# The first phase of an FFT-filter and bilinear kernel put into one list of single steps

## The chip, the cores and the metric

The kernel runs on one core of a Trainium2 chip. The metric is the time of one execution on the device, in microseconds. PE is TensorE, DVE is VectorE, ACT is ScalarE, POOL is GpSimd and SP is SyncE, which here only issues transfers.

## The reference

```python
X = np.fft.rfft(x, axis=1)                 # x: (8, 3072, 256) float32
F = (filt_r + 1j * filt_i)[None, :, :]
y = np.fft.irfft(X * F, n=3072, axis=1).astype(np.float32)
h = y.reshape(8 * 3072, 256)
out = ((h @ w_a) * (h @ w_b) @ w_out).astype(np.float32)   # d_ff = 1536
```

The three weights arrive as float64, 8 bytes per element.

## The kernel before

**The main loop.** A batch (3072 rows) is worked on as 6 chunks (c) of 4 x 128 rows, and each chunk against 6 pairs of column blocks (p). `pair` does one of these 288 units. It makes seven products per weight (`term`, L577, three matmuls each, a high and a low part of every operand), adds them on VectorE (`add`, L627), multiplies the two sides (`g`, L649, L652, L661), splits `g` into a high part on ScalarE and a low part on GpSimd (`parts`, L586), and multiplies it by `w_out` in the next unit (`project`, L594). While a batch is in this loop, the FFT of the next one is put between the units by `plan` and `early`, two tables of slots; a unit has two slots.

**The first phase** is what must come ahead of the first unit: the FFT, the filter and the inverse FFT of batch 0, and as many weights as are needed at once. It is written in lines 684 to 723.

- Stage one has 12 steps: `first_x` loads 256 KB of x, `first_s1` multiplies it by a table on TensorE, ScalarE copies the result out of PSUM (L483) into one of two buffers `z`, and ScalarE's queue stores it to DRAM (L484).
- Stage two has 16 steps, which read DRAM in another order, so every store of stage one must have landed: `first_z` loads 192 KB (L494), `first_f` a tile of the filter (L488, real rows in partitions 0 to 63, imaginary rows in 64 to 127), `first_s2` multiplies by a table (L500), then by the filter. On VectorE that is two multiplications of 64 rows by the real part (L510, L511) and one by the imaginary part (L512). The fourth goes over ScalarE (L513, a negated copy) and GpSimd (L514). `first_is1` transforms back and stores 192 KB to `td`.
- `first_tt` (L535) loads the part of `td` that the first unit needs, and `is2` (L544) makes the first chunk from it, with L548 as its first matmuls.

**The weights** come as 18 items of 512 columns, in threes: `w_a`, `w_b` and `w_out` for each p. An item is loaded as raw words (`conv_load`, 512 KB), and its float64 bits are turned into a float32 value and a remainder. `conv_expo` masks the exponent (VectorE), `conv_scale` makes a power of two from it (ScalarE, twice, in PSUM), `conv_parts` does four operations on VectorE, `conv_split` adds the low word on GpSimd, `conv_combine` makes four sums of blocks on VectorE (L304, only for `w_a` and `w_b`), copies the high part on ScalarE and subtracts it on GpSimd. `more_weights` calls all six for six successive items; one call is a tick.

```python
for stage, lag in ((conv_combine, 5), (conv_split, 4), (conv_parts, 3), (conv_scale, 2), (conv_expo, 1), (conv_load, 0)):
    if 0 <= t - lag < len(conv):
        stage(conv[t - lag])
```

Fifteen ticks stand in the first phase. The other eight stand in slots 0 to 7 of batch 0 (L740 to L742), one in each slot, that is in the first four units.

**What sets the order.** `tc.manual_schedule()` takes the instructions as they are written: each engine works through its own in that order, and waits where an operand or a buffer isn't ready. The transfers of SP go out in their written order too, and a transfer that waits for a buffer holds back those behind it.

## Time and profile before

| | us |
|---|---|
| median of 3 runs | 2661.36 (2660.98 to 2662.94) |
| the profiled execution, its own time | 2662.36 |
| its span, first to last instruction | 2660.6 |
| busy: PE, DVE, ACT, POOL | 2589.5, 1665.2, 1412.2, 1321.8 |

The page of the profile gives shares over the whole span. The change lies in the first 180 us, so the views by window, by group and by time of that stretch are the ones to read. In the timeline a line is one instruction or a run of the same, with its start, its length, and in brackets how long the engine was idle ahead of it and what ended that.

### The profile page before, as it was taken

What the parts mean: (1) busy time and instruction counts of PE and PEld (TensorE: products, weight loads), DVE (VectorE), ACT (ScalarE), POOL (GpSimd) and SP (SyncE); (2) the same over time, 40 slices, a digit from 0 to 9 for tenths busy, and PEclk for the clock granted to TensorE, in tenths of its full rate; (3) what the DMA queues carried; (4) which work ended last, traced back from release to release, by engine and by line L of the source; (5) the groups of instructions that cost most, each with busy time, mean ns of one, the idle gap of its engine ahead of it and who ended that gap; (6) DMA issues with size and microseconds to landing.
All of it is one profiled execution on the core that took longest, in us unless ns stands there. A gap on an engine that the chain in (4) does not pass through costs nothing.

```text
span 2660.6 us, 54030 instructions
## 1 busy us (share of the span) xinstructions
PE 2589.5 (97%) x20920; PEld 2518.2 (95%) x20920; DVE 1665.2 (63%) x2648; ACT 1412.2 (53%) x2630; POOL 1321.8 (50%) x1044
## 2 busy tenths in 40 slices
PE   5789999999999999999999999999999999999999
PEld 2389999999999999999999999999999999999998
DVE  5775785558845687456865478545884468744443
ACT  3456555555555555555555555555555555545444
POOL 3575454545545555454545545454454545434333
PEclk6899999999999999999999999999999999999999
DMA  7626441344324443244423454234432444311000
GB/s 248 181 98 223 141 135 62 127 150 137 113 74 136 158 137 97 78 163 136 145 66 112 139 154 139 66 119 156 132 120 66 144 152 141 94 33 33 29 21 17
DMA packets 213634, 310.88 MB, mean 117 GB/s; under 512 B 21393, under 2 KB 121298, under 8 KB 213330
## 3 DMA queue, kind: packets, MB, share of 16 engines
q1 hardware_dynamic: 184882, 278.85, 32.7%
q10 hardware_dynamic: 28496, 28.58, 3.5%
q8 instruction: 164, 2.69, 0.4%
q14 instruction: 92, 0.75, 0.1%
HBM read 202.49 MB, written 108.00 MB: 117 GB/s over the span
## 4 chain that ended last, share of the span: by engine, by line
PE 88%; POOL 4%; DVE 3%; issue 2%; DMA 2%; ACT 1%; SPq 0%; ACTq 0%; POOLq 0%; DVEq 0%
PE po L603 10%; PE ps_p L582 10%; PE ps_p L583 9%; PE ps_p L584 9%; PE po L601 9%; PE po L602 9%; PE ps_r L584 5%; PE ps_r L582 5%; PE ps_r L583 5%; PE ps L548 3%; PE ps_q L582 2%; PE ps_q L584 2%; PE ps_q L583 2%; PE ps L361 2%; POOL xol L567 2%
## 5 line engine op out<-in xcount | busy, mean ns | idle before, releaser
L591 POOL TENSOR_TENSOR gl<-g,gh 128x512 fp32r<-128x512 f32 x576 | 747.1, 1297 | 959.2 <-ACT gh L590 894.7
L601 PE MATMUL po<-woh,gh 128*128 128x256 f32 x2304 | 656.1, 285 | 0.0
L603 PE MATMUL po<-woh,gl 128*128 128x256 f32 x2304 | 649.7, 282 | 3.1 <-POOL gl L591 1.1
L590 ACT CAST gh<-g 128x512 fp32r<-128x512 f32 x576 | 358.9, 623 | 550.6 <-DVE g L649 532.0
L602 PE MATMUL po<-wol,gh 128*128 128x256 f32 x2304 | 645.9, 280 | 0.0
L627 DVE TENSOR_TENSOR cs<-ps_r,s 128x512 f32<-128x512 f32 x288 | 199.1, 691 | 450.6 <-PE ps_r L584 397.0
L623 ACT COPY s<-ps_p 128x512 f32<-128x512 f32 x576 | 338.0, 587 | 242.5 <-PE ps_p L584 205.9
L603 PEld LDWEIGHTS po<-woh,gl 128*128 128x128 f32 x2304 | 433.8, 188 | 7.8 <-POOL gl L591 7.8
L601 PEld LDWEIGHTS po<-woh,gh 128*128 128x128 f32 x2304 | 434.9, 189 | 3.1
L602 PEld LDWEIGHTS po<-wol,gh 128*128 128x128 f32 x2304 | 434.7, 189 | 2.9
L582 PE MATMUL ps_p<-xoh,wah 128*128 128x256 f32 x1152 | 326.0, 283 | 12.0 <-DVE cs L627 7.6
L584 PE MATMUL ps_p<-xol,wbh 128*128 128x256 f32 x1152 | 323.9, 281 | 0.0
L583 PE MATMUL ps_p<-xoh,wal 128*128 128x256 f32 x1152 | 323.6, 281 | 0.0
L584 PE MATMUL ps_p<-xol,wah 128*128 128x256 f32 x1152 | 323.1, 280 | 0.0
L582 PE MATMUL ps_p<-xoh,wbh 128*128 128x256 f32 x1152 | 322.7, 280 | 0.0
L583 PE MATMUL ps_p<-xoh,wbl 128*128 128x256 f32 x1152 | 322.6, 280 | 0.0
L627 DVE TENSOR_TENSOR cs<-ps_q,s 128x512 f32<-128x512 f32 x288 | 199.1, 691 | 187.0 <-PE ps_q L584 161.4
L649 DVE TENSOR_TENSOR g<-cs 128x512 f32<-128x512 f32 x288 | 300.9, 1045 | 6.1 <-POOL gl L591 6.1
L567 POOL TENSOR_TENSOR xol<-xf,xoh 128x256 fp32r<-128x256 f32 x192 | 246.9, 1307 | 20.9 <-ACT xoh L566 20.9
L661 DVE TENSOR_TENSOR g<-ps_p,cs 128x256 f32<-128x256 f32 x288 | 122.1, 424 | 213.2 <-ACT cs L660 210.2
L442 POOL TENSOR_TENSOR yl<-y,yh 128x512 fp32r<-128x512 f32 x112 | 144.3, 1289 | 223.7 <-ACT yh L441 223.7
L582 PEld LDWEIGHTS ps_p<-xoh,wah 128*128 128x128 f32 x1152 | 217.5, 189 | 13.8 <-DVE cs L627 8.5
(125 smaller groups left out, 6239.1 us busy)
## 6 DMA issues: line engine op xcount, KB each, us to landing
filt<-in_filt SPq DMA_DIRECT2D x336, 128.0 KB, 2.8
z<-zh SPq DMA_DIRECT2D x112, 256.0 KB, 3.0
zt<-z SPq DMA_DIRECT2D x112, 256.0 KB, 3.0
td<-t ACTq DMA_DIRECT2D x128, 192.0 KB, 2.2
out<-ot SPq DMA_DIRECT2D x95, 256.0 KB, 2.1
tt<-td SPq DMA_DIRECT2D x47, 512.0 KB, 4.2
xt<-in_x SPq DMA_DIRECT2D x84, 256.0 KB, 2.9
st<-s1d SPq DMA_DIRECT2D x84, 256.0 KB, 3.4
```

What stands on the lines that cost most here:

```text
L567: nc.gpsimd.tensor_tensor(out=xl[:, o], in0=xf[:, i], in1=f32(xh[:, o]), op=ALU.subtract)
L582: nc.tensor.matmul(o, wh[:, p, w], xh[:, i], start=first and h == 0, stop=False, skip_group_check=True)
L583: nc.tensor.matmul(o, wl[:, p, w], xh[:, i], start=False, stop=False, skip_group_check=True)
L584: nc.tensor.matmul(o, wh[:, p, w], xl[:, i], start=False, stop=True, skip_group_check=True)
L590: nc.scalar.copy(out=gh, in_=g[:, f])
L591: nc.gpsimd.tensor_tensor(out=gl, in0=g[:, f], in1=f32(gh), op=ALU.subtract)
L601: nc.tensor.matmul(o, gh[:, ts], woh[:, n], start=n == 0 and j % 2 == 0, stop=False, skip_group_check=True)
L602: nc.tensor.matmul(o, gh[:, ts], wol[:, n], start=False, stop=False, skip_group_check=True)
L603: nc.tensor.matmul(o, gl[:, ts], woh[:, n], start=False, stop=n == NF - 1, skip_group_check=True)
L623: nc.scalar.copy(out=s, in_=bank)
L627: nc.vector.tensor_tensor(out=cs[:, :, n], in0=bank, in1=s, op=ALU.add)
L649: nc.vector.tensor_tensor(out=g[:, 0].rearrange("p (t n) -> p t n", t=2), in0=cs[:, 0, 0:2], in1=cs[:, 1, 0:2], op=ALU.mult)
```

## The change

- **One list.** The first phase is no longer written as loops with ticks between, but as `FIRST`, a list of 289 single steps in one order. A letter is a function, the number its item or step: `g x k s z w` are stage one (`z` the copy out of PSUM, `w` the store, now issued by SP), `Z f S y n v I t T` stage two, `r o a c h l j q` the eight steps of one weight item. Items 0 to 11 are done in it, and items 12 to 15 are loaded.
- **Conversion.** `conv_open` masks the exponent and, in a second operation with two scalars, takes the mantissa and sets its leading bit, then adds the low word times 2^-32 (L275). `conv_close` puts the sign into the scale and multiplies (two operations). The addition on GpSimd and two operations on VectorE go; the four block sums move from VectorE to GpSimd (L326).
- **Filter.** The real filter is loaded into both halves of the rows (`filt_r`, 256 KB), the imaginary part into rows 64 to 127 (`filt_i`, 128 KB). VectorE does one multiplication of 128 rows (L555) and one of 64 (L556). The later batches load the filter in this layout too, with two transfers where there were three.
- **Buffers.** The result of stage one has one place in SBUF for all 12 steps, in memory that weights use later; 13 input tiles instead of 8; five sets of filter tiles for steps 0 to 9, two for the rest.
- **Main loop.** Items 12 to 17 are opened in slots 0, 1, 3, 4, 6 and 7 and done by slot 9, over five units.

```diff
+FIRST = """
+g0 x0 x1 x2 r0 g1 x3 x4 x5 r1 s0 g2 x6 x7 s1 z0 x8 r2 s2 z1 w0 g3 o0 z2 w1 x9 w2 x10 s3 x11 a0 k s4 r3 s5 z3
...
+w10 o3 w11 l2 j1 q1 a3 c3 h3 Z0 l3 f0 Z1 f1 Z2 S0 f2 j3 Z3 n0 Z4 q3 y0 Z5 S1 Z6 Z7 v0 n1 Z8 y1 Z9 S2 Z10 v1
+Z11 I0 n2 y2 Z12 r4 v2 f3 I1 t0 f4 T0 r5 f5 I2 t1 f6 T1 r6 S3 f7 S4 r7 n3 Z13 o4 S5 Z14 n4 Z15 S6 v3 y3 v4 a4
...
+c10 r13 h9 t15 l9 o11 r14 h10 T15 a11 j9 c11 q9 r15 h11 l10 l11 j10 q10
+"""
...
+    def conv_open(w):
...
+        v.tensor_scalar(out=e, in0=hw, scalar1=0x7FF00000, scalar2=None, op0=ALU.bitwise_and)
+        v.tensor_scalar(
+            out=m, in0=hw, scalar1=0xFFFFF, scalar2=0x100000, op0=ALU.bitwise_and, op1=ALU.bitwise_or
+        )
+        v.scalar_tensor_tensor(
+            out=f32(m), in0=lw.bitcast(U32), scalar=2.0 ** -32, in1=m, op0=ALU.mult, op1=ALU.add
+        )
...
+    def conv_close(w):
+        raw, _, m, sc = w[3:]
+        nc.vector.scalar_tensor_tensor(
+            out=sc, in0=raw[:, :, 1], scalar=-(1 << 31), in1=sc, op0=ALU.bitwise_and, op1=ALU.bitwise_or
         )
...
+        nc.vector.scalar_tensor_tensor(
+            out=f32(m), in0=f32(m), scalar=2.0 ** -20, in1=f32(sc), op0=ALU.mult, op1=ALU.mult
         )
...
-    def conv_split(w):
...
-        nc.gpsimd.tensor_tensor(out=m, in0=m, in1=f32(dst_h), op=ALU.subtract)
-        nc.gpsimd.tensor_tensor(out=dst_l, in0=m, in1=f32(lo), op=ALU.add)
...
-            nc.vector.tensor_tensor(out=s[:, o], in0=a, in1=b, op=op)
...
+            nc.gpsimd.tensor_tensor(out=s[:, o], in0=a, in1=b, op=op)
...
+        nc.sync.dma_start(out=z0[:, 2 * i:2 * i + 2], in_=firsts["z"][:, 2 * i:2 * i + 2])
...
+        n = i % 5 if i < 10 else i % 2
...
+        nc.sync.dma_start(out=fr_, in_=filt_r[:, 2 * i:2 * i + 2])
+        nc.sync.dma_start(out=fm[64:128], in_=filt_i[:, 2 * i:2 * i + 2])
...
-        nc.vector.tensor_tensor(out=y[0:64], in0=ps[0:64], in1=ft[0:64], op=ALU.mult)
-        nc.vector.tensor_tensor(out=y[64:128], in0=ps[64:128], in1=ft[0:64], op=ALU.mult)
-        nc.vector.tensor_tensor(out=v[64:128], in0=ps[0:64], in1=ft[64:128], op=ALU.mult)
...
+        nc.vector.tensor_tensor(out=y, in0=ps, in1=fr_, op=ALU.mult)
+        nc.vector.tensor_tensor(out=v[64:128], in0=ps[0:64], in1=fm[64:128], op=ALU.mult)
...
-                left = len(conv) + 5 - tick[0]
-                for i in range(left):
-                    at(i, more_weights)
...
+                for i, t in enumerate((0, 1, 3, 4, 6, 7), len(conv) - 6):
+                    for fn, lag in zip(CONV[1:], (0, 0, 1, 1, 2, 2, 2)):
+                        at(t + lag, fn, conv[i])
+                    if i + 4 < len(conv):
+                        at(t + 2, conv_load, conv[i + 4])
```

**SP, where stage two begins.** `z_98` and `z_94` are the DRAM tensor between the stages, `raw` the words of a weight item, `filt`, `f` the filter. Before:

```order
L245 DMA raw<-in_wb 128x2x512
L494 DMA zf<-z_98 96x2x256
L488 DMA filt_95<-in_filt 128x512
L494 DMA spare<-z_98 96x2x256
L488 DMA filt_96<-in_filt 128x512
L494 DMA spare<-z_98 96x2x256 x2
L245 DMA raw<-in_wo 128x2x512
```

In the changed kernel:

```order
L529 DMA zf<-z_94 96x2x256
L537 DMA f_289<-in_fr 128x512
L538 DMA f_289<-in_fm 64x512
L529 DMA zf<-z_94 96x2x256 x5
L529 DMA spare<-z_94 96x2x256 x5
L261 DMA raw<-in_wb 128x2x512
L537 DMA f_289<-in_fr 128x512
L538 DMA f_289<-in_fm 64x512
```

After the filter tile of step 2, ten loads of `z` and a weight item now stand ahead of the filter tile of step 3; before, loads of `z` and of the filter alternated.

**VectorE, in the middle of stage two.** `y`, `v` are the products with the filter, `e`, `m`, `sc` belong to a weight item. Before:

```order
L512 TENSOR_TENSOR v_387<-ps,filt_94 64x512
L270 SCALAR_TENSOR_TENSOR sc<-raw,sc 128x512
L273 TENSOR_SCALAR m<-raw 128x512
L274 SCALAR_TENSOR_TENSOR m<-m,sc 128x512
L277 SCALAR_TENSOR_TENSOR e<-raw,sc 128x512
L250 TENSOR_SCALAR e<-raw 128x512
L510 TENSOR_TENSOR y_412<-ps,filt_95 64x512
L511 TENSOR_TENSOR y_412<-ps,filt_95 64x512
L512 TENSOR_TENSOR v_413<-ps,filt_95 64x512
```

In the changed kernel:

```order
L556 TENSOR_TENSOR v_335<-ps,f_289 64x512
L271 TENSOR_SCALAR e<-raw 128x512
L272 TENSOR_SCALAR m<-raw 128x512
L275 SCALAR_TENSOR_TENSOR m<-raw,m 128x512
L555 TENSOR_TENSOR y_395<-ps,f_289 128x512
L556 TENSOR_TENSOR v_396<-ps,f_289 64x512
L555 TENSOR_TENSOR y_400<-ps,f_289 128x512
L556 TENSOR_TENSOR v_401<-ps,f_289 64x512
L293 SCALAR_TENSOR_TENSOR sc<-raw,sc 128x512
L296 SCALAR_TENSOR_TENSOR m<-m,sc 128x512
```

A filter step takes two instructions instead of three, and an item comes in two halves with filter steps between them.

**VectorE, from one unit of the main loop to the next.** `cs` and `g` belong to the unit. Before, from the second unit to the third:

```order
L661 TENSOR_TENSOR g<-ps_p,cs 128x256
L304 TENSOR_TENSOR s<-m 128x128
L304 TENSOR_TENSOR s<-s,m 128x128
L304 TENSOR_TENSOR s<-m 128x128
L304 TENSOR_TENSOR s<-m,s 128x128
L270 SCALAR_TENSOR_TENSOR sc<-raw,sc 128x512
L273 TENSOR_SCALAR m<-raw 128x512
L274 SCALAR_TENSOR_TENSOR m<-m,sc 128x512
L277 SCALAR_TENSOR_TENSOR e<-raw,sc 128x512
L250 TENSOR_SCALAR e<-raw 128x512
L627 TENSOR_TENSOR cs<-ps_q,s 128x2x256
```

In the changed kernel, from the first unit to the second:

```order
L722 TENSOR_TENSOR g<-ps_p,cs 128x256
L293 SCALAR_TENSOR_TENSOR sc<-raw,sc 128x512
L296 SCALAR_TENSOR_TENSOR m<-m,sc 128x512
L271 TENSOR_SCALAR e<-raw 128x512
L272 TENSOR_SCALAR m<-raw 128x512
L275 SCALAR_TENSOR_TENSOR m<-raw,m 128x512
L688 TENSOR_TENSOR cs<-ps_q,s 128x2x256
L293 SCALAR_TENSOR_TENSOR sc<-raw,sc 128x512
L296 SCALAR_TENSOR_TENSOR m<-m,sc 128x512
L688 TENSOR_TENSOR cs<-ps_r,s 128x2x256
```

Between the last `g` of a unit and the first addition of the next stand five instructions instead of nine; one more item is closed ahead of the second addition.

## Rows read from the trace of the kernel before

**Rows 1.** page, section 1: busy us, share of the span, instructions of each engine

```profile
PE 2589.5 (97%) x20920; PEld 2518.2 (95%) x20920; DVE 1665.2 (63%) x2648; ACT 1412.2 (53%) x2630; POOL 1321.8 (50%) x1044
```

**Rows 2.** busy us of each engine in stretches of 20 us

```profile
core 0: us, PE busy (x) PEld busy (x) DVE busy (x) ACT busy (x) POOL busy (x), PEclk, DMA share, GB/s
60.00:80.00 20.00, 15.64 (x33) 6.48 (x32) 19.45 (x31) 8.90 (x16) 11.76 (x10) 0.84 0.66 197
80.00:100.00 20.00, 18.11 (x36) 6.51 (x34) 19.45 (x31) 10.52 (x19) 13.17 (x12) 0.87 0.81 237
...
160.00:180.00 20.00, 18.12 (x139) 17.66 (x138) 18.20 (x32) 10.11 (x22) 15.48 (x14) 0.91 0.05 11
180.00:200.00 20.00, 20.00 (x172) 20.00 (x171) 9.15 (x17) 11.28 (x23) 12.20 (x11) 1.00 0.32 106
```

**Rows 3.** timeline: start us, us, engine, line, operation; the first stage and its end

```profile
9.81 0.43 DVE L250 TENSOR_SCALAR e<-raw 128x512 int32<-128x512 int32 x1 [8.91 <-DMA raw<-in_wa]
...
34.17 0.58 ACT L483 COPY z<-ps 128x512 f32<-128x512 f32 x1 [4.89 <-DMA z<-z]
...
45.69 0.35 SPq L494 DMA_DIRECT2D zf<-z  x1
...
112.21 0.68 DVE L512 TENSOR_TENSOR v<-ps,filt 64x512 f32<-64x512 f32 x1
...
120.37 0.46 SPq L535 DMA_DIRECT2D tt<-td  x1
...
124.19 3.75 PE L548 MATMUL ps<-gt,tt 128*128 128x128 f32 x16 [6.70 <-issue]
```

**Rows 4.** waits from 0 to 130 us: us in total, times, longest

```profile
ACT z L483 <- DMA z<-z: 10.8, 5, 4.9
```

**Rows 5.** DMA from 3 to 26 us, all queues

```profile
DMA packets 4461, 8.41 MB, mean 366 GB/s; under 512 B 553, under 2 KB 778, under 8 KB 4461
```

**Rows 6.** groups by form, 0 to 125 us: busy us, mean ns, idle before

```profile
L250 DVE TENSOR_SCALAR e<-raw 128x512 int32<-128x512 int32 x14 | 11.7, 834 | 16.1 <-DMA raw<-in_wa 10.0 <-DMA raw<-in_wo 5.2 <-DMA raw<-in_wb 0.9
L510 DVE TENSOR_TENSOR y<-ps,filt 64x512 f32<-64x512 f32 x16 | 10.9, 680 | 0.3
L274 DVE SCALAR_TENSOR_TENSOR m<-m,sc 128x512 int32<-128x512 int32 x12 | 8.3, 688 | 0.4
L273 DVE TENSOR_SCALAR m<-raw 128x512 int32<-128x512 int32 x12 | 6.8, 562 | 0.1
L304 DVE TENSOR_TENSOR s<-m 128x128 f32<-128x128 f32 x14 | 4.3, 306 | 7.6 <-ACT z L483 5.1 <-POOL m L285 2.4
L307 POOL TENSOR_TENSOR wal<-m,wah 128x128 fp32r<-128x128 f32 x4 | 2.0, 491 | 13.1 <-ACT wah L305 12.9
L310 POOL TENSOR_TENSOR wal<-s,wah 128x512 fp32r<-128x512 f32 x4 | 5.3, 1313 | 0.0
```

**Rows 7.** page, section 5: VectorE on a PSUM tile of 128 rows

```profile
L627 DVE TENSOR_TENSOR cs<-ps_r,s 128x512 f32<-128x512 f32 x288 | 199.1, 691 | 450.6 <-PE ps_r L584 397.0
```

**Rows 8.** DMA issues from 0 to 130 us: KB each, median us to landing

```profile
filt<-in_filt SPq DMA_DIRECT2D x16, 256.0 KB, 3.9
```

**Rows 9.** timeline: VectorE's product g, once in each pair of column blocks

```profile
138.85 0.68 DVE L649 TENSOR_TENSOR g<-cs 128x512 f32<-128x512 f32 x1
...
176.03 1.44 DVE L649 TENSOR_TENSOR g<-cs 128x512 f32<-128x512 f32 x1
...
199.87 0.68 DVE L649 TENSOR_TENSOR g<-cs 128x512 f32<-128x512 f32 x1
```

**Rows 10.** groups by form on VectorE, 124 to 180 us

```profile
L250 DVE TENSOR_SCALAR e<-raw 128x512 int32<-128x512 int32 x4 | 5.5, 1388 | 0.0
```

**Rows 11.** timeline: two records of the second stage's matmuls

```profile
101.98 1.91 PE L500 MATMUL ps<-v,icf 128*96 128x512 f32 x2
...
103.69 1.91 PE L500 MATMUL ps<-zf,fcf 96*128 96x512 f32 x2
```

**Rows 12.** the same stretch: busy us by engine as in Rows 2, granted clock

```profile
102.00:104.00 2.00, 2.00 (x3) 0.91 (x4) 1.92 (x4) 1.21 (x3) 1.26 (x1) 0.53 0.68 198
```

More of the change, by code (lines that the diff above doesn't have):

```diff
@@ L296, in conv_combine, with conv_low @@
             return
         m = m.rearrange("p (k f c) -> p k f c", k=2, f=2)
+        wh = wt[p][:, 2 * h]
+        nc.scalar.copy(out=wh[:, 0], in_=m[:, 0, 0])
+        nc.scalar.copy(out=wh[:, 1:3], in_=m[:, 1])
+    def conv_low(w):
+        p, h, m = w[1], w[2], w[-1]
+        sub = lambda out, a, b: nc.gpsimd.tensor_tensor(out=out, in0=a, in1=f32(b), op=ALU.subtract)
+        if h is None:
+            wh, wl = (t[:, 2 * p:2 * p + 2].rearrange("p f d -> p (f d)") for t in (woh, wol))
+            sub(wl, m, wh)
+            return
+        m = m.rearrange("p (k f c) -> p k f c", k=2, f=2)
+        wh, wl = wt[p][:, 2 * h], wt[p][:, 2 * h + 1]
@@ L389, in load_f @@
         fr, fm = filts[2 * (i % 2)], filts[2 * (i % 2) + 1]
-        for h in range(2):
-            nc.sync.dma_start(out=fr[half[h]], in_=filt[half[0], 2 * i:2 * i + 2])
-        nc.sync.dma_start(out=fm[half[1]], in_=filt[half[1], 2 * i:2 * i + 2])
+        nc.sync.dma_start(out=fr, in_=filt_r[:, 2 * i:2 * i + 2])
+        nc.sync.dma_start(out=fm[half[1]], in_=filt_i[:, 2 * i:2 * i + 2])
     def load_z(b, i):
@@ L463, in first_in @@
         if not spare:
[L464 to L465 removed]
+            spare.extend(p2.tile([128, 3, 2, D], F32, name="spare", tag="xol") for _ in range(2))
+        n = taken[0] % 13
         taken[0] += 1
[L467 removed]
+        return fr.tile([128, 2, D], F32, name=name, tag="in", bufs=7) if n < 7 else spare[(n - 7) // 3][:, (n - 7) % 3]
     def first_x(i):
@@ L480, in first_s1, with first_out_z, first_turned @@
         for n in range(2):
-            nc.tensor.matmul(ps[:, n], sf[:, 2 * (i % 4) + n], xt[:, n], start=True, stop=True)
-        z = fr.tile([128, 2, D], F32, name="z0", tag="z0", bufs=2)
-        nc.scalar.copy(out=z, in_=ps)
-        nc.scalar.dma_start(out=z0[:, 2 * i:2 * i + 2], in_=z)
-    def first_f(i):
-        ft = filts[i % NFT]
-        nc.sync.dma_start(out=ft, in_=filt[:, 2 * i:2 * i + 2])
-        held["f0", i] = ft
-    def first_z(i):
+            nc.tensor.matmul(ps[:, n], sf[:, 2 * (i % 6) + n], xt[:, n], start=True, stop=True)
+        held["s0", i] = ps
+    def first_z(i):
+        if i == 0:
+            firsts["z"] = const.tile([128, 7168], F32, name="z0", tag="w45")[:, :N2 * D].rearrange("p (n d) -> p n d", n=N2)
+        nc.scalar.copy(out=firsts["z"][:, 2 * i:2 * i + 2], in_=held.pop(("s0", i)))
+    def first_out_z(i):
+        nc.sync.dma_start(out=z0[:, 2 * i:2 * i + 2], in_=firsts["z"][:, 2 * i:2 * i + 2])
+    def first_turned(i):
         zt = first_in("zf")
@@ L579, in term @@
         xh, xl = held["xo", b, c]
-        for h, (wh, wl) in enumerate(((wah, wal), (wbh, wbl))):
-            o = bank[:, h]
-            nc.tensor.matmul(o, wh[:, p, w], xh[:, i], start=first and h == 0, stop=False, skip_group_check=True)
-            nc.tensor.matmul(o, wl[:, p, w], xh[:, i], start=False, stop=False, skip_group_check=True)
-            nc.tensor.matmul(o, wh[:, p, w], xl[:, i], start=False, stop=True, skip_group_check=True)
+        for h in range(2):
+            o, wh, wl = bank[:, h], wt[p][:, 2 * h, w], wt[p][:, 2 * h + 1, w]
+            nc.tensor.matmul(o, wh, xh[:, i], start=first and h == 0, stop=False, skip_group_check=True)
+            nc.tensor.matmul(o, wl, xh[:, i], start=False, stop=False, skip_group_check=True)
+            nc.tensor.matmul(o, wh, xl[:, i], start=False, stop=True, skip_group_check=True)
     def parts(u, f):
```

213 lines of the change are left out of this document (101 added, 112 removed).

## Prediction

> **What bounds the kernel now.** I began with the shares of the whole span: TensorE is busy 97% of it [rows 1], so time can come back only where it isn't. The table of 20 us stretches says where that is [rows 2]. From 180 us on TensorE is busy 20.00 of 20 us, and only fewer matmuls could shorten that; the change leaves them alone. Ahead of it two parts are slow. From 60 to 100 us VectorE is busy 19.45 of every 20 us, and in 160 to 180 it is at 18.20, while TensorE idles there. So all that the change can win or lose lies in the first 180 us, and a microsecond by which the saturated loop starts earlier is a microsecond of the total.
>
> The timeline gives the marks [rows 3]. Stage one ends where the first load of z is issued, at 45.69; the last product with the filter ends at 112.89 (112.21 + 0.68); the first matmul of the first chunk starts at 124.19. The tail between these last two is 11.3 us. The main loop then needs until about 180 to run at its own pace.
>
> One measurement of this kernel can tell a change from none at about 0.2%, that is 5.3 us; the chances at the end use that bound.
>
> **Stage one: 45.7 to about 31 us.** What held it was the two buffers for z: ScalarE waited 10.8 us, in five waits, for a store to finish before it could copy out the next result [rows 4], one of them 4.89 us [rows 3]. All twelve results now have a place, so these waits go. What is late next is the transfers. Up to the first load of z the list moves 4 tables of 384 KB, 12 tiles of x of 256 KB, 4 weight items of 512 KB, 192 KB of small tables and 12 stores of 256 KB: 9920 KB, or 10.2 MB. From 3 to 26 us the queues moved 366 GB/s on average [rows 5], and at that rate 10.2 MB take 27.8 us. From the 3 us of the first stretch that is 31 us. The conversion of items 0 to 3 fits beside it: 4 items at the 3.5 us worked out below are 14 us of VectorE. Gain of this part: 14.7 us. The bounds: 28 us if the transfers lose nothing at the start, 36 us if the stores wait on SP behind loads as they did on ScalarE's queue half of the time.
>
> **Stage two: 67.2 us (45.7 to 112.9) to about 66.** Three resources come close together here, and I priced each.
>
> *VectorE.* A weight item took 0.83 + 3 x 0.69 + 0.56 = 3.46 us, and the sums 4 x 0.31 = 1.2 us more for two items in three [rows 6]. Now it is two masks and three operations of 0.69 us. The second mask has two scalars, which no row shows; its bounds are the 0.56 us of L273, which it replaces, and the 0.69 us of an operation with two tensors [rows 6]. I take 0.7 for each mask, so 3.5 us: the item itself isn't cheaper, only its sums leave. The filter took three operations of 0.68 us per step [rows 6]. The 128-row product is new; that 64 rows cost 0.68 and 128 rows from PSUM cost 0.69 [rows 7] says that rows are free, so a step now takes 1.38 us instead of 2.05. Eight items are left for stage two: 8 x 3.5 + 16 x 1.38 = 50 us. To that I add 8 us of idleness: ten loads of z and one item stand ahead of the filter tile of step 3, 2.5 MB, which is 8 us at the 295 GB/s below, and the three steps before it can't fill it. That gives 58 us.
>
> *Transfers.* From the first load of z to the last filter tile: 16 loads of 197 KB, 16 filter steps of 393 KB (262 before), 10 items of 524 KB, 14 stores of 197 KB and 0.65 MB for the first chunk: 18.1 MB. In stage two the queues moved 197 GB/s at a share of 0.66 and 237 at 0.81 [rows 2], so 295 GB/s at a full share; that is 61 us, and 65 us at a share of 0.95. The wider filter itself costs 2.1 MB of this, 7 us.
>
> *TensorE.* Three matmuls of 512 columns per step. At the lower of its two clock levels one took 1.71 us, the distance of two records [rows 11], where the granted clock was 0.53 [rows 12]; at the full one it takes half, 0.86. So 48 of them need 41 to 82 us, and at the 0.85 that was granted between 60 and 100 us [rows 2] about 48.
>
> The largest counts, the transfers: 65 us and one last product. Stage two alone wins a microsecond, because what VectorE gives back is asked for by the larger loads. The last product ends at 31 + 66 = 97 us, and with the old tail of 11.3 us the first chunk starts at about 108, 16 us earlier than now. The four sums that go to GpSimd cost there 4 x 0.49 us per item [rows 6], against 1.3 us for the addition that leaves it, so 0.7 us more for two items in three, and 1.3 us less for the third, where one of two subtractions goes: in total nothing. What hides it is that GpSimd was busy 13.2 of 20 us at most in this stage [rows 2]. If that cover were gone, 0.7 us would be paid for each of eight items, 5 us.
>
> **The first units of the loop.** The product g comes once in a unit. The first three intervals took 37.2 us (138.85 to 176.03), the next three 23.8 (176.03 to 199.87) [rows 9]; with the tick of some 4 us ahead of the first g about 17 us go here. VectorE takes them. In 180 to 200 us it was busy 9.15 us [rows 2] for 20/7.9 = 2.5 units, 3.6 us a unit; two ticks of 4.3 us (an item and its share of the sums) make that 12.2, and an interval was 12.4. A tick now doesn't come in every slot. Per interval the new table gives one opening and two closings, two and one, one and one, one and two, a closing being 1.4 us and an opening 0.69 us and two masks. A mask took 1.39 us here [rows 10]; for the pair I take 1.9, the second at the 0.56 of its forerunner [rows 6]. With the unit's 3.6 us that is 9.0, 10.2, 7.6 and 9.0 us. VectorE got no further than 18.20 us of work in 20 here [rows 2], a share of 0.91, so 9.9, 11.2, 8.4 and 9.9 against 7.9: 8 us lost, about 10 with the first unit. Gain: 7 us, between 2 (both masks at 1.39) and 12 (both at the 0.43 of the first one of all [rows 3]).
>
> **A rule that speaks against this.** The trace shows masks of 0.83 us on average in the first phase and of 1.39 us in the loop [rows 6, 10], so something besides their own length delays them. The Trainium skill, "SBUF — State Buffer", in the section "SBUF: two separate sides", says that VectorE, in a two-port mode or with two inputs in SBUF, and GpSimd share a pair of ports which one of them holds for a whole instruction while the other is fully blocked. By that rule two masks an item and four more operations on GpSimd are the wrong trade; the trace agrees as far as a mask's 0.43, 0.83 and 1.39 us go, and the second rival below is what it would cost if each mask met one.
>
> **The sum.** The profiled execution took 2662.4 us, 1.0 over the median of the runs and 1.8 over its span. 16 + 7 = 23 us less is 2639; against the median 2638.
>
> **Rivals.**
>
> - *The transfers go no faster than they did.* At the best 20 us of stage two, 237 GB/s [rows 2], 18.1 MB take 76 us; the first chunk starts at 120, and 4 + 7 us are won: 2650. For it: loads wait for buffers as before. Against it: more tiles, so deeper prefetch. Chance 0.15.
> - *GpSimd blocks VectorE.* If each mask waits for one 1.31 us operation of GpSimd [rows 6] on top of the 0.43 of the first mask [rows 3], the 16 masks of stage two cost 16 x 1.04 = 17 us more, VectorE needs 75 us instead of 58, 9 more than the forecast's 66, and the loop's gain is gone: 2654. For it: the masks of the loop at 1.39. Against it: in stage two VectorE was busy 97% and GpSimd some 60% [rows 2], and the mean was still 0.83. Chance 0.06.
> - *TensorE's clock stays low.* If shorter bursts keep it at the lower level, 48 x 1.71 = 82 us [rows 11] from the first z at 34 us, then a store of 3.9 us [rows 8] and the 3.8 us from the last load to the first chunk [rows 3]: the first chunk at 124, nothing won ahead of the loop and 7 us in it, 2654. Chance 0.06.
> - *VectorE paces all of it, with no idleness.* Stage two is 50 us plus 3 for the first load, the transfers keep 340 GB/s, the tail stays; the first chunk starts near 96, and with 10 us in the loop 38 us are won: 2623. Chance 0.12.
> - *One queue in single file: slower.* SP takes its list in order, and a load that waits for a buffer (only two filter sets after step 9, four item buffers) stops all behind it. A filter load lands 3.9 us after its issue [rows 8]. Each that goes out only when its user is already waiting adds that to the path. The 23 us are gone after six, and if all 16 filter loads and 10 items do it, 26 x 3.9 = 101 us stand in place of 65: 13 us slower than now, 2674. For it: the tile of step 12 needs the products of step 10 done. Against it: ten steps have five sets. Chance 0.07.
>
> **The numbers.** Forecast 2638, chance 0.54 with its bounds: stage one 5 us late and the loop's low end give 2648, stage one at 28 us and its high end 2630. The range reaches from the VectorE rival to the low clock, 2621 to 2654, and leaves out the slower rival and the far ends, about 0.15. Faster by over 0.2% is everything below 2656: the forecast, the first and fourth rival, and most of the second and third, 0.89. Within 0.2%: the rest of these two and the single file half way, 0.06. Slower: 0.05.
>
> **What would show it.** The first load of z near 31 us, the first chunk near 108, TensorE full from about 156; no wait of ScalarE for stores of z; a 128-row filter product at 0.69 us; a DMA share above 0.9 between 35 and 90 us. It is wrong if stage two gets shorter by more than 5 us (then the transfers weren't the bound), if the first load of z comes after 36, or if units still take over 12 us.

## The result, and the profile after

The changed kernel took 2677.25 us (median of 4 runs, 2674.43 to 2678.83), the kernel before 2662.15 beside it: a ratio of 1.0055, with a 95% interval of 1.0038 to 1.0073. It is 15 us slower, more than the 0.2% that a measurement can tell; 2638 was forecast. The profiled execution took 2675.81 us, its span is 2674.0.

The first phase did what was forecast of it, nearly. The timeline of the changed kernel, with the marks of [rows 3] and three of the products g of [rows 9]:

```profile
30.77 0.34 SPq L529 DMA_DIRECT2D spare<-z  x1
...
100.20 0.68 DVE L556 TENSOR_TENSOR v<-ps,filt 64x512 f32<-64x512 f32 x1
...
111.06 2.26 PE L609 MATMUL ps<-gt,tt 128*128 128x128 f32 x9 [7.29 <-DMA tt<-td]
...
123.61 0.68 DVE L710 TENSOR_TENSOR g<-cs 128x512 f32<-128x512 f32 x1
...
183.38 0.69 DVE L710 TENSOR_TENSOR g<-cs 128x512 f32<-128x512 f32 x1 [1.87 <-POOL gl L652]
...
384.64 1.52 DVE L710 TENSOR_TENSOR g<-cs 128x512 f32<-128x512 f32 x1
```

The first g comes 15.2 us earlier than before (138.85), the sixth 8.7 us earlier (183.38 against 192.10), the 29th 6.9 us earlier. That one stands in the timeline of the kernel before at

```profile
391.55 1.53 DVE L649 TENSOR_TENSOR g<-cs 128x512 f32<-128x512 f32 x1
```

At the end the lead of 6.9 us has become a lag of 13.4 (spans 2674.0 and 2660.6). So 6.5 us went in the five units from the first g to the sixth, 1.8 from there to the 29th, and 20.3 between 390 us and the end, where nothing was thought to change. The windows show that second loss. The columns are those of [rows 2]; the number in the first pair of brackets counts TensorE's products. The kernel before, 1000 to 2000 us:

```profile
1000.00:2000.00 1000.00, 997.96 (x8251) 985.28 (x8250) 653.00 (x1011) 544.47 (x1014) 507.10 (x393) 1.00 0.38 121
```

The changed kernel, with the stretches of [rows 2] ahead of it:

```profile
60.00:80.00 20.00, 13.52 (x24) 4.41 (x24) 16.92 (x23) 9.57 (x18) 13.07 (x15) 0.83 0.86 261
80.00:100.00 20.00, 14.16 (x33) 5.14 (x31) 17.19 (x22) 13.51 (x24) 15.61 (x19) 1.00 0.81 250
160.00:180.00 20.00, 16.78 (x117) 16.59 (x118) 12.61 (x20) 11.91 (x24) 13.48 (x15) 0.83 0.13 40
180.00:200.00 20.00, 18.34 (x153) 18.13 (x152) 8.46 (x15) 10.03 (x20) 10.74 (x9) 1.00 0.40 127
1000.00:2000.00 1000.00, 999.10 (x8182) 986.49 (x8181) 646.18 (x1002) 540.41 (x1004) 502.72 (x390) 1.00 0.39 121
```

TensorE is busy 99.9% of the last stretch, at the full granted clock, and completes 8182 products where it completed 8251: 0.84% fewer. Over the 2280 us after the 29th g that is 19 us, nearly all of the 20.3. Same products, same clock, no idle time, and still slower: the busy share can't show such a loss, the count in a stretch does.

Beside the filter steps of the later batches, what differs in the loop is where the operands lie. Of a product's two operands one is loaded first and held (a weight of 128x128, or a block of g), the other is streamed past it (a part of x, or of the output weights, 128x256). The compiled programs give the addresses; *modulo 512* is what is left of an address when multiples of 512 bytes are taken off. In both kernels the streamed parts of x start at byte 288 modulo 512 of their partition (124704), and g's parts at 480. The weights started at 128 (1152 and multiples of 512 from there); the new tiles are allocated as they are needed, behind the small tables, and start at 288 (38688). The output weights start at 128 in both. The runs on the rate of the loop and on the other operands move some of these.

The waits from 112 to 195 us (us in total, times, longest) tell of the first loss:

```profile
ACT w L333 <- POOL s L326: 10.6, 4, 4.7
...
PE ps_p L643 <- ACT s L684: 7.3, 2, 4.7
...
PE ps L609 <- DVE m L296: 3.3, 1, 3.3
```

Two records of the timeline belong together, ScalarE's rounding of the sums and, three instructions behind it, the copy that TensorE waits for:

```profile
139.89 0.62 ACT L333 CAST w<-s 128x512 fp32r<-128x512 f32 x1 [4.71 <-POOL s L326]
```

```profile
142.36 0.58 PE L643 MATMUL ps_p<-xoh,w 128*128 128x256 f32 x1 [4.72 <-ACT s L684]
```

### The profile page after: what moved, and what is told of

The parts are those of the page before. It is cut to its first block, busy times and chain, and to the rows that moved or that the text cites. A ratio compares the mean times of both kernels' runs of the same rounds, so it can differ in the third digit from the quotient of the medians.

```text
span 2674.0 us, 53770 instructions
## 1 busy us (share of the span) xinstructions
PE 2607.9 (98%) x20920; PEld 2539.5 (95%) x20920; DVE 1643.5 (61%) x2584; ACT 1412.7 (53%) x2630; POOL 1322.7 (49%) x1074
## 4 chain that ended last, share of the span: by engine, by line
PE 93%; DMA 3%; POOL 2%; DVE 1%; issue 1%; ACT 1%; SPq 0%; POOLq 0%; DVEq 0%; ACTq 0%
PE po L664 10%; PE ps_p L645 10%; PE po L662 10%; PE ps_p L643 10%; PE ps_p L644 10%; PE po L663 10%; PE ps_r L645 5%; PE ps_r L643 5%; PE ps_r L644 5%; PE ps L609 3%; PE ps_q L645 2%; PE ps_q L643 2%; PE ps_q L644 2%; PE ps L386 2%; PE ps L432 2%; PE ps L431 2%
## 5 line engine op out<-in xcount | busy, mean ns | idle before, releaser
L643 PE MATMUL ps_p<-xoh,w 128*128 128x256 f32 x2304 | 651.1, 283 | 10.0 <-ACT s L684 7.3
L645 PE MATMUL ps_p<-xol,w 128*128 128x256 f32 x2304 | 652.2, 283 | 0.3 <-POOL xol L628 0.3
L644 PE MATMUL ps_p<-xoh,w 128*128 128x256 f32 x2304 | 651.8, 283 | 0.0
L643 PEld LDWEIGHTS ps_p<-xoh,w 128*128 128x128 f32 x2304 | 439.8, 191 | 11.8 <-ACT s L684 8.4
L662 PEld LDWEIGHTS po<-woh,gh 128*128 128x128 f32 x2304 | 440.7, 191 | 3.0
L645 PEld LDWEIGHTS ps_p<-xol,w 128*128 128x128 f32 x2304 | 440.0, 191 | 0.5 <-POOL xol L628 0.5
L644 PEld LDWEIGHTS ps_p<-xoh,w 128*128 128x128 f32 x2304 | 440.1, 191 | 0.0
L645 PE MATMUL ps_r<-xol,w 128*128 128x256 f32 x1152 | 326.6, 284 | 1.8 <-POOL xol L628 1.8
L643 PE MATMUL ps_r<-xoh,w 128*128 128x256 f32 x1152 | 325.4, 282 | 0.0
L644 PE MATMUL ps_r<-xoh,w 128*128 128x256 f32 x1152 | 325.1, 282 | 0.0
```

Of the source, the lines that this page charges most:

```text
L643: nc.tensor.matmul(o, wh, xh[:, i], start=first and h == 0, stop=False, skip_group_check=True)
L644: nc.tensor.matmul(o, wl, xh[:, i], start=False, stop=False, skip_group_check=True)
L645: nc.tensor.matmul(o, wh, xl[:, i], start=False, stop=True, skip_group_check=True)
L662: nc.tensor.matmul(o, gh[:, ts], woh[:, n], start=n == 0 and j % 2 == 0, stop=False, skip_group_check=True)
```

## The experiments: the rate of the loop

Line numbers of a version may lie one to three above those of the changed kernel. *Distance* is the start of the streamed x less that of the held weights, modulo 512: 160 before, 0 after the change.

**Run 1, the changed kernel, weights 32 bytes further.** x comes 64 further, to 352.

```diff
-    sct = const.tile([128, 2], F32, name="sct")
+    sct = const.tile([128, 16], F32, name="sct")[:, 0:2]
             wt[p], wt[p + 1] = t[:, 0], t[:, 1]
+            const.tile([128, 8], F32, name="pad")
```

> The changed kernel with its six weight tiles 32 bytes further on, so that each starts at a multiple of 64 bytes of its partition's memory as it did before the change; every product's other operand keeps its place modulo 64. Address theory (the 32-byte offset of the weights slows each term product by about 1.5 ns): 1000 to 2000 us holds about 8250 products again (before 8251, changed 8182), the weight loads' median is 188 ns instead of 192, the time is 2650 to 2660 us. Layout theory (high and low part of a weight now 3584 bytes apart instead of 21504): nothing moves, 8180 products, 192 ns, 2677 us. Phase theory (something that the new first phase leaves behind, or other work beside the products): 2677 us as well.

2643.67 us, ratio to before 0.9933 [0.9920, 0.9945]. Faster than the 2650 to 2660 us of the address theory, with 8291 products:

```profile
1000.00:2000.00 1000.00, 997.27 (x8291) 983.91 (x8290) 652.16 (x1011) 547.88 (x1018) 508.29 (x394) 1.00 0.38 121
```

Unused bytes alone give 33 us, where the layout and the phase theory gave nothing.

**Run 2, the kernel before, its weights at 32 modulo 64.**

```diff
+    const.tile([128, 8], F32, name="pad0")
     wah = const.tile([128, NP, 7, 128], F32R, name="wah")
...
     wbl = const.tile([128, NP, 7, 128], F32R, name="wbl")
+    const.tile([128, 8], F32, name="pad1")
```

> The kernel before with its four weight tiles 32 bytes further on, at 32 modulo 64, everything else at its old place modulo 64. Address theory: about 18 to 24 us slower, 2680 to 2686 us, with about 8180 products from 1000 to 2000 us and weight loads of 192 ns. Layout theory and phase theory: 2662 us, 8250 products, 188 ns.

2641.36 us, 0.9923 [0.9910, 0.9935]: 21 us faster where 20 us slower was expected. The weights' own start is not the rule.

**Run 3, the changed kernel, weights and x both 32 bytes further**, by the first edit of run 1 alone.

```diff
-    sct = const.tile([128, 2], F32, name="sct")
+    sct = const.tile([128, 16], F32, name="sct")[:, 0:2]
```

> The changed kernel with all that lies behind the scale table 32 bytes further on: the weights at a multiple of 64 as in the first run, and besides the parts of x that stream through the products, the forward tables and the spectra. Address theory if only the held operand counts: as the first run, 2650 to 2660 us. If the streamed operand's start counts too: faster than the first run, 2625 to 2645 us, with more than 8300 products from 1000 to 2000 us. Layout and phase theory: 2677 us.

2674.70 us, 1.0052 [1.0038, 1.0065], 8184 products: no gain, where the address theories gave 2625 to 2660 us. Weights and x moved together, the distance stayed 0.

**Run 4, the kernel before with the same edit**, which there moves x and not the weights.

> The kernel before with all that lies behind the scale table 32 bytes further on; its weights were at a multiple of 64 already, the streamed parts of x come to one. If only the held operand's start counts: 2662 us. If the streamed operand's counts too: 2635 to 2650 us. Layout and phase theory: 2662 us.

2638.96 us, 0.9913 [0.9900, 0.9927], 8322 products. Together the four runs contradict every theory about one operand's start; what they do fit is the distance. The next five vary it and leave the weights, the output weights and g's parts where they were. What lies behind x, the operands of the next batch's transform, moves along with x.

**Run 5, the changed kernel, x 64 bytes further.**

```diff
             wt[p], wt[p + 1] = t[:, 0], t[:, 1]
+            const.tile([128, 16], F32, name="pad")
```

> The first four runs fit no rule of the weights' own start; they fit the distance from a weight to the streamed part of x, taken modulo some power of two: distance 0 modulo 512 (the changed kernel, and again with all 32 bytes further) 19038 and 19044 products from 300 to 2620 us; 32: 19313; 160 (before): 19207; 192 (both shifted versions of before): 19379 and 19386. Here the streamed operands alone lie 64 bytes further than in the changed kernel, the weights stay at 32 modulo 64: distance 64. Distance theory: 19300 to 19390 products, 2630 to 2645 us. Theory of the weights' own start (32 modulo 64 slow): 2677 us, 19040 products. Theory that the number is an accident of each build and tied to no address: anything between 2635 and 2677 us.

2635.73 us, 0.9900 [0.9884, 0.9917], 8320 products from 1000 to 2000 us. The distance theory gave 2630 to 2645.

**Runs 6 and 7, x 128 and 256 bytes further.**

```diff
+            const.tile([128, 32], F32, name="pad")
```

> The streamed operands alone 128 bytes further than in the changed kernel: distance 128. If the distance counts modulo 128, this is as bad as distance 0: about 19040 products from 300 to 2620 us, 2677 us. If it counts modulo 256 or 512, it is as good as 32 to 192: 19200 to 19390 products, 2632 to 2655 us.

```diff
+            const.tile([128, 64], F32, name="pad")
```

> The streamed operands alone 256 bytes further: distance 256. If the distance counts modulo 128 or 256: about 19040 products, 2677 us. If modulo 512: 19200 to 19390 products, 2632 to 2655 us.

2665.73 us with 8218 products at 128, 2679.85 with 8184 at 256. Distance 256 is as bad as 0, and 128 has come a quarter of the way from there to the 8320 of run 5: neither quite a rule modulo 128, by which it would be as slow as 0, nor one modulo 256.

**Run 8, the kernel before, x 352 bytes further**, so that its distance becomes 0.

```diff
     nyq = const.tile([128, D], F32, name="nyq")
+    const.tile([128, 88], F32, name="pad")
```

> The kernel before, streamed operands alone 352 bytes further, so that its distance goes from 160 to 512, 0 modulo 512; its weights stay at multiples of 64, its layout and its first phase stay as they were. Distance theory: the slow rate, about 19040 products from 300 to 2620 us instead of 19207, 2680 to 2688 us. Layout theory (the slow rate belongs to the changed kernel's weight tiles) and the theory of the weights' own start: 2662 us or faster.

2676.28 us, 1.0053 [1.0038, 1.0068]: the kernel before becomes as slow as the changed one, by 352 bytes that nothing reads. It came out 4 us under the expected range, with

```profile
1000.00:2000.00 1000.00, 998.63 (x8203) 986.53 (x8202) 648.62 (x1006) 542.40 (x1008) 504.19 (x391) 1.00 0.38 121
```

**Run 9, the changed kernel at the distance of before, 160.** This is the change less its shift of addresses.

```diff
+            const.tile([128, 40], F32, name="pad")
```

> The changed kernel with the streamed operands 160 bytes further, so that its distance from weights to streamed operand is the 160 of the kernel before: the change less its shift of addresses. Distance theory: the rate of before, about 19195 products from 300 to 2620 us against 19028 in the changed kernel, so 2460 us of loop less 0.87%, 21 us: 2655 us, faster than before by the lead of about 7 us that the changed kernel still had when its loop was full. If the distance counts only modulo 128, 160 is as good as 32: 19300 products, 2642 us. If the slow loop were the new first phase's or the layout's doing: 2677 us.

2653.90 us, 0.9974 [0.9963, 0.9984], with the rate of before:

```profile
1000.00:2000.00 1000.00, 998.03 (x8257) 985.12 (x8256) 651.02 (x1009) 546.01 (x1015) 507.52 (x393) 1.00 0.39 120
```

So, with the old distance, what the change was written to do is worth 7.6 us (2661.45 beside it); the shift of addresses cost 23.4 on top (2677.25 less 2653.90).

## The experiments: the first units

All of these start from run 5 (2635.73 us), where the five units from the first g to the sixth take 59.4 us (124.33 to 183.77; before 53.25, 138.85 to 192.10). The whole times of runs 10 to 13 lie within 3.5 us of run 5's, less than the 0.2% (5.3 us) that a measurement can tell. What these runs show, they show in their traces, each of one execution.

**Run 10, the sums that are made in the loop, back on VectorE.**

```diff
-            nc.gpsimd.tensor_tensor(out=s[:, o], in0=a, in1=b, op=op)
+            (nc.vector if streaming else nc.gpsimd).tensor_tensor(out=s[:, o], in0=a, in1=b, op=op)
```

> From the changed kernel with distance 64 (2635.7 us): the sums of the two last pairs' weights, which are made in the loop's first units, go back to VectorE; those of the first phase stay on GpSimd. Theory that ScalarE's rounding of the sums waits for GpSimd (11.5 us of waiting in the first units) and holds up the copies that TensorE needs: the second to the sixth unit take 53 to 55 us instead of 59.4, and the end comes 4 to 6 us earlier, 2630 us. Rival, VectorE's queue sets the first units and the sums lengthen it: no gain or up to 4 us slower, 2636 to 2640 us.

2638.50 us, 0.9909 [0.9896, 0.9923]. That is in the range of the rival. The five units fell to 57.9 us, and ScalarE now waited for VectorE instead (waits, 112 to 190 us):

```profile
ACT w L334 <- DVE s L327: 7.8, 4, 2.7
```

**Run 11, the rounding of the sums half a unit later.**

```diff
-                    for fn, lag in zip(CONV[1:], (0, 0, 1, 1, 2, 2, 2)):
+                    for fn, lag in zip(CONV[1:], (0, 0, 1, 1, 2, 3, 3)):
```

> From the same kernel: the sums stay on GpSimd, but ScalarE's rounding of them and what follows it stand half a unit later in the order of issue. Theory of the waiting ScalarE: as good as the sums on VectorE or better, 2629 to 2631 us, and ScalarE's wait for the sums gone. Rival (GpSimd's own work sets the first units): the wait only moves, 2635 us.

2638.17 us, 0.9910 [0.9897, 0.9924]; five units in 57.9 us. ScalarE's wait for the sums is no longer among the long waits, but only 1.5 us of units came of it and nothing of the end. The theory of the waiting ScalarE explains little of the 6 us. One unit still took 14.2 us, and the timeline of this run shows it, TensorE's turn of the next chunk between two products g:

```profile
160.00 1.28 DVE L711 TENSOR_TENSOR g<-cs 128x512 f32<-128x512 f32 x1
...
164.09 2.08 PE L610 MATMUL ps<-gt,tt 128*128 128x128 f32 x8 [2.98 <-DVE m L297]
...
174.22 1.19 DVE L711 TENSOR_TENSOR g<-cs 128x512 f32<-128x512 f32 x1
```

The turn needs a PSUM bank that a conversion's scale still holds, and VectorE frees it behind the unit's own products. The windows of the same run show what follows the pause: TensorE is busy throughout, at a granted clock of 0.50, the lower of its two levels (1.2 GHz), with 25 products in 5 us; at the full level there are 172 in 20 us [rows 2].

```profile
160.00:165.00 5.00, 1.99 (x11) 1.69 (x11) 4.29 (x8) 2.13 (x6) 3.23 (x4) 0.81 0.01 2
165.00:170.00 5.00, 5.00 (x25) 5.00 (x25) 1.96 (x5) 2.86 (x5) 0.06 (x1) 0.50 0.52 156
```

The changed kernel has the same wait, the 3.3 us for L296 above. Stretches at a lower clock are no mark of the change: the kernel before has 32 products in 160 to 165 us, at a granted clock of 0.66.

**Run 12, all sums back on VectorE, in the first phase too.**

```diff
-            nc.gpsimd.tensor_tensor(out=s[:, o], in0=a, in1=b, op=op)
+            nc.vector.tensor_tensor(out=s[:, o], in0=a, in1=b, op=op)
```

> From the same kernel: all sums on VectorE, in the first phase too (the part of the change that moved them, undone). The forecast put them at 14.7 us of VectorE's time in the first phase, and the transfers at nearly the same length there: if the forecast was right in that, the last filter product ends 0 to 10 us later than the 100.9 us of the changed kernel. If the order of steps was made for sums on GpSimd and VectorE is now the longer, 10 to 15 us later.

2639.21 us. The last filter product ends at 103.48 (102.79 + 0.69), against 102.49 in run 5 (101.80 + 0.69): one microsecond later. 24 of the sums stand ahead of it, and from 3 to 103 us VectorE was busy 65.55 us, 58.86 in run 5. So 6.7 us more of VectorE's work cost 1 us: VectorE was not what set the end of stage two. Both products waited for their part of the filter. Run 5, then run 12:

```profile
101.80 0.69 DVE L557 TENSOR_TENSOR v<-ps,filt 64x512 f32<-64x512 f32 x1 [0.23 <-DMA filt<-in_fm]
```

```profile
102.79 0.69 DVE L557 TENSOR_TENSOR v<-ps,filt 64x512 f32<-64x512 f32 x1 [0.26 <-DMA filt<-in_fm]
```

**Run 13, run 11 with the last conversion one slot later**, so that no scale is issued ahead of the turn in slot 7.

```diff
-                for i, t in enumerate((0, 1, 3, 4, 6, 7), len(conv) - 6):
+                for i, t in enumerate((0, 1, 3, 4, 6, 8), len(conv) - 6):
```

> From the kernel with distance 64 and the rounding of the sums half a unit later (2638.2 us): the last of the six conversions in the loop's first units starts in slot 8 instead of slot 7, so that the turn of the next chunk in slot 7 no longer takes a PSUM bank that a conversion's last product on VectorE has to free. Theory (this wait of 3.0 us, and the half granted clock behind it, make the unit of 14.2 us): the unit falls to 8 to 10 us, the end comes 4 to 6 us earlier, 2632 to 2634 us. Rival (the first units are set by the sum of the work on ScalarE and VectorE): the next unit grows by as much, 2637 to 2639 us.

2633.88 us, 0.9892 [0.9876, 0.9908]: 4.3 us less than run 11, in the forecast range, though the two intervals overlap. The unit of 14.2 us became one of 10.4 (8 to 10 expected); the next grew from 10.0 to 11.5. In the timeline and the windows the wait and the low clock are gone:

```profile
158.28 1.28 DVE L711 TENSOR_TENSOR g<-cs 128x512 f32<-128x512 f32 x1
...
159.23 1.05 PE L610 MATMUL ps<-gt,tt 128*128 128x128 f32 x8
...
168.71 1.29 DVE L711 TENSOR_TENSOR g<-cs 128x512 f32<-128x512 f32 x1
```

```profile
160.00:165.00 5.00, 4.04 (x35) 3.85 (x34) 3.23 (x7) 3.66 (x9) 3.02 (x3) 1.00 0.51 161
165.00:170.00 5.00, 4.65 (x39) 4.45 (x38) 4.97 (x8) 2.79 (x5) 4.92 (x8) 1.00 0.00 0
```

Part of the 4.3 us is chance: the first g of run 13 came 1.75 us earlier than that of run 11 (124.59 and 126.34), and nothing ahead of it differs. The five units went from 57.9 to 55.7 us.

## The experiments: the other operands

**Run 14, run 5 with everything from the output weights on 32 bytes further.**

```diff
+    const.tile([128, 8], F32, name="pad0")
     woh = const.tile([128, NF, D], F32R, name="woh")
```

> From the changed kernel with distance 64 (2635.7 us): everything from the output weights on lies 32 bytes further, so that the distance from g's parts (held) to the output weights (streamed) goes from 32 to 64 modulo 128, while that of the term products stays 64. Distance theory for any pair of a held and a streamed operand: the output products go from about 120.5 ns apart to 116 to 118, so 6912 of them times 3 to 4 ns, 20 to 26 us: 2610 to 2616 us. Rival, the distance counts for the term products alone, or the modulus is no 128: 2636 us.

2643.10 us, 0.9932 [0.9919, 0.9945], with 8286 products: 7 us slower where 20 us faster was expected. The weights and x had moved too, to 320 and 384, at the same distance. The starts of TensorE's records from 1000 to 2000 us tell the two kinds of product apart. The output products did gain: on average they start 119.3 ns apart, 120.8 in run 5. The term products lost more: 118.3 ns, 116.5 in run 5. So the distance is not all of the rule.

**Run 15, both edits of runs 13 and 14.**

> Both edits together, the later last conversion and the output weights 32 bytes further: the sum of the two gains if both theories hold, 2605 to 2612 us; 2636 if neither does.

2638.30 us, 0.9912 [0.9898, 0.9927]: 4.8 us less than run 14. It has run 11's edit too, and the same two edits took 1.9 us off run 5 (2635.73 to 2633.88). The five units take 53.5 us, as many as before the change. The term products start 118.3 ns apart, as in run 14, and the sum of two gains did not come.

**Run 16, the kernel before with the edit of run 14.** Weights stay at 128, x comes to 320, the output weights to 160.

> The kernel before with everything from the output weights on 32 bytes further: its term products' distance goes from 160 to 192, its output products' from 32 to 64 modulo 128. With the first alone it took 2639 us. Distance theory: 20 to 26 us less, 2613 to 2619 us. Rival as for the output products above: 2639 us.

2613.44 us, 0.9816 [0.9802, 0.9830], in the expected range and 25.5 us less than run 4, which differs in the start of the output weights (and of four small tables) alone. The output products start 117.9 ns apart, 121.9 in run 4, and the term products 115.3 and 115.7:

```profile
1000.00:2000.00 1000.00, 995.61 (x8421) 982.61 (x8420) 658.96 (x1022) 550.82 (x1026) 511.78 (x397) 1.00 0.38 120
```

**Run 17, run 13 with all four groups at run 16's places modulo 256**: weights at 384 modulo 512, x at 64, output weights at 160, g's parts at 480.

```diff
+            tables["ict"] = const.tile([128, 3, 96], F32R, name="ict")
+            const.tile([128, 16], F32, name="pad1")
...
+    sct = const.tile([128, 2], F32, name="sct")
     woh = const.tile([128, NF, D], F32R, name="woh")
...
-    ict = const.tile([128, 3, 96], F32R, name="ict")
-    sct = const.tile([128, 2], F32, name="sct")
...
     nyq = const.tile([128, D], F32, name="nyq")
+    const.tile([128, 56], F32, name="pad0")
```

> The changed kernel with the later last conversion, and with the weights, the streamed parts of x, the output weights and g's parts at the same places modulo 256 as in the fastest version of the kernel before (2613.4 us; its products' rate 8421 from 1000 to 2000 us, against 8286 in the changed kernel with the output weights moved alone). If these places alone set the loop's rate: the same rate, 8400 to 8430 products, and the lead of the first phase on top, 2603 to 2610 us, the fastest of all. If the arrangement of the changed kernel's tiles (high and low part interleaved) has a price of its own: 8280 to 8350 products, 2625 to 2645 us.

2598.95 us (2596.26 to 2600.00), 0.9761 [0.9748, 0.9775]: the fastest, 63 us under the kernel before, with the rate of run 16:

```profile
1000.00:2000.00 1000.00, 994.26 (x8433) 981.66 (x8433) 654.84 (x1019) 553.67 (x1032) 514.88 (x401) 1.00 0.39 121
```

The same places gave nearly the same rate in two kernels with different tiles and different first phases. The lead over run 16 is 14.5 us, more than the 3 to 10 expected.

The starts modulo 512, the distance, products from 1000 to 2000 us, the mean ns from the start of a term product to that of a term product right behind it (and the same for output products), and the time:

| version | weights | x | output weights | distance | products | term | output | us |
|---|---|---|---|---|---|---|---|---|
| changed | 288 | 288 | 128 | 0 | 8182 | 119.6 | 121.8 | 2677.3 |
| run 3 | 320 | 320 | 128 | 0 | 8184 | 120.0 | 121.1 | 2674.7 |
| run 7 | 288 | 32 | 128 | 256 | 8184 | 119.6 | 121.7 | 2679.9 |
| run 8, before | 128 | 128 | 128 | 0 | 8203 | 119.9 | 120.1 | 2676.3 |
| run 6 | 288 | 416 | 128 | 128 | 8218 | 119.2 | 121.1 | 2665.7 |
| before | 128 | 288 | 128 | 160 | 8251 | 118.2 | 121.4 | 2662.2 |
| run 9 | 288 | 448 | 128 | 160 | 8257 | 118.3 | 120.7 | 2653.9 |
| run 14 | 320 | 384 | 160 | 64 | 8286 | 118.3 | 119.3 | 2643.1 |
| run 1 | 320 | 352 | 128 | 32 | 8291 | 117.4 | 120.7 | 2643.7 |
| run 5 | 288 | 352 | 128 | 64 | 8320 | 116.5 | 120.8 | 2635.7 |
| run 4, before | 128 | 320 | 128 | 192 | 8322 | 115.7 | 121.9 | 2639.0 |
| run 2, before | 160 | 352 | 192 | 192 | 8326 | 115.6 | 121.9 | 2641.4 |
| run 16, before | 128 | 320 | 160 | 192 | 8421 | 115.3 | 117.9 | 2613.4 |
| run 17 | 384 | 64 | 160 | 192 | 8433 | 115.1 | 117.7 | 2599.0 |

With the output weights at 128, distances that are multiples of 128 are the slow ones, 32 more is better, 64 more best. The term products alone follow the distance in this way, with run 14 as the one exception. Runs 14 and 16 show that the rest of the addresses counts as well. Runs 10 to 13, at run 5's places, had 8306 to 8312 products, so differences of some 15 say nothing.

## Why the prediction was wrong

**The step that failed** is in the first paragraph: "From 180 us on TensorE is busy 20.00 of 20 us, and only fewer matmuls could shorten that; the change leaves them alone." The change left the products alone and moved their operands, and so took 0.84% off the rate of a loop of 2400 us. I read the diff for instructions and queues, and not for the allocations: the tiles that were now made one by one behind the small tables were in it. Run 9, with the old distance, took 2653.9 us; the shift of addresses is the 23 us on top. That is only just within the range of 2621 to 2654, and 16 us over the forecast, so the address was not the only miss. Of the lead of 23 us that was forecast, the traces lack 2.9 us at the first chunk and 11.4 more at the sixth g; another 22.1 went after it.

**The first units** were a second wrong term. The lead was 13.1 us at the first chunk, 15.2 at the first g and 8.7 at the sixth: 4.4 us lost where 7 were to be won. Two of the five units took 15.2 and 14.5 us (133.27 to 148.49, 158.83 to 173.29), over the 12 that the prediction named as a sign of being wrong, and TensorE was full only from 185 us on, not from 156. I took VectorE's work as the bound there, and its masks were not even priced too low. The two masks, groups by form from 113 to 185 us, took 1.39 us where 1.9 was taken:

```profile
L271 DVE TENSOR_SCALAR e<-raw 128x512 int32<-128x512 int32 x6 | 4.4, 740 | 0.0
...
L272 DVE TENSOR_SCALAR m<-raw 128x512 int32<-128x512 int32 x6 | 3.9, 645 | 0.0
```

VectorE was busy 12.61 us of the 20 from 160 to 180, where it had been 18.20 [rows 2]. What took the time was the order: a bank freed late, ScalarE held by sums, and TensorE at half its clock after the pause. Of the 6 us by which run 5's five units exceed those of before, runs 10 and 11 give 1.5 to the waiting ScalarE and run 13 another 2.2 to the bank and the clock, each from one trace. With both edits runs 15 and 17 took 53.5 and 53.2 us, what it was before the change, where run 13 took 55.7. So the two edits account for 3.7 to 6.2 us together, and how much is whose stays open. The sentence on the sums that go to GpSimd, "in total nothing", holds for its busy time (1322.7 us, 1321.8 before) and leaves out who stands behind the wait.

**Stage one** was right: the first load of z at 30.77, forecast 31, and no wait for a store of z.

**Stage two** took 70.1 us (30.77 to 100.88), forecast 66. The product over 128 rows cost what was said, and so did the second mask, 0.73 us against 0.7. The addition L275 did not: 1.00 us where 0.69 was taken (groups by form, 0 to 113 us):

```profile
L275 DVE SCALAR_TENSOR_TENSOR m<-raw,m 128x512 f32<-128x512 uint32 x12 | 12.0, 996 | 0.4
L272 DVE TENSOR_SCALAR m<-raw 128x512 int32<-128x512 int32 x12 | 8.7, 728 | 0.0
...
L555 DVE TENSOR_TENSOR y<-ps,filt 128x512 f32<-128x512 f32 x10 | 6.9, 688 | 11.4 <-ACT xi L567 7.7 <-DMA filt<-in_fr 2.6 <-PE ps L544 1.0
...
L271 DVE TENSOR_SCALAR e<-raw 128x512 int32<-128x512 int32 x12 | 6.7, 555 | 20.2 <-DMA raw<-in_wa 10.5 <-DMA raw<-in_wb 7.1 <-DMA raw<-in_wo 2.4
```

The transfers did not keep the 0.95 that was assumed: 0.86 and 0.81 from 60 to 100 us, 0.88 over all of stage two:

```profile
30.77:100.88 70.11, 50.84 (x99) 18.78 (x100) 46.47 (x64) 32.12 (x57) 39.61 (x44) 0.84 0.88 254
```

That VectorE's work was no longer the bound is shown by run 12. What the queue lost shows at the end of the stage (timeline of SP):

```profile
88.37 0.42 SPq L261 DMA_DIRECT2D raw<-in_wa  x1
94.29 0.34 SPq L596 DMA_DIRECT2D tt<-td  x1
94.68 0.46 SPq L537 DMA_DIRECT2D filt<-in_fr  x1
```

From 88.37 to 94.29 SP issued nothing more. The load of `tt` waited for stores of `td` (5.4 us in two waits), and behind it stands the real part of the filter for the last step, for which VectorE then waited 2.03 us (99.48). No run moved that load, so that it cost the 4 us over the forecast is argued and not shown. With a tail of 10.2 us the first chunk started at 111.06, forecast 108: 13 of 16 us were won.

**The rivals.** The slower one, a queue in single file, has the sign and not the size: stage two came out 4 us over the forecast, not 36, and the slower end came from the loop. The one that let GpSimd block VectorE was wrong in size. In the first phase the two masks took 0.56 and 0.73 us on average, in the loop 0.74 and 0.65, where one mask alone had taken 0.83 and 1.39 [rows 6, 10]. In stage two the 14 masks lost 4.3 us against the shortest of them (0.43 and 0.41), not the 17 of the rival, and seven additions L275 another 3.4 against 0.69. But the delay is there. Five of these operations took 1.48 to 1.64 us; each began 0.13 to 0.35 us after one of GpSimd and ended 0.28 to 0.55 us after it, as these two (timeline):

```profile
94.13 1.36 POOL L338 TENSOR_TENSOR w<-s,w 128x512 fp32r<-128x512 f32 x1
94.28 1.49 DVE L272 TENSOR_SCALAR m<-raw 128x512 int32<-128x512 int32 x1
```

The rule behind it (the Trainium skill, "SBUF — State Buffer", section "SBUF: two separate sides") agrees with these five. It cost little because VectorE's work was not the bound. No rival spoke of the loop's rate, so the range was too narrow by its lack.

## What to carry to other kernels

When a change touches tiles, compare the addresses of the operands that the saturated engine reads, before and after, and count its instructions in a stretch of the steady loop: a busy share of 99.9% hides a loss of 1%. When two versions are timed, vary the placement by some unused bytes before crediting or blaming the code: here 32 bytes were worth up to 49 us, more than the whole change. For a crowded stretch, add up who waits for whom and not only busy time, and count the clock that TensorE loses after a pause.

## What the runs showed of the hardware that was not expected

TensorE's rate depends on where its operands lie in a partition's memory. The same list of products, busy 99.4 to 99.9% at a granted clock of 1.00, came to between 8182 and 8433 in 1000 us, 3.1% apart. The start of the weights against that of the streamed x goes with 1.7% of it (8182 to 8322), a shift of the output weights by 32 bytes with another 1.2% (8322 to 8421). Term products start 115.1 to 120.0 ns apart and output products 117.7 to 121.9, by these places.

The section of the Trainium skill named above says that within the engine side only the port pair of VectorE and GpSimd causes contention, and that TensorE's ports wait for nobody. What TensorE waits for here, and whether another engine has a part in it, no run shows. That the places of its own operands change its rate, runs 4 to 9 and 16 do, so for this loop the measurement decides.

Open is the whole rule. Run 14 has a distance of 64 and completes 0.4% fewer products than run 5 with the same distance; only in it, in run 15 and in run 8 does x start at a multiple of 128. No run tried that alone, and run 8 is no slower than runs 3 and 7 at distances 0 and 256. Runs 14 and 17 have the output weights and g's parts at the very same bytes, and their output products start 119.3 and 117.7 ns apart. Which pair of operands meets, whether held against streamed or another, and over which period, was not separated.
